# Loads between passes in order of need, one weight's conversion in the third pass, and Strassen products that accumulate on a copy in PSUM

## The chip, the cores and the metric

One core of a Trainium2 chip runs the whole kernel. The metric is the device time of one execution in microseconds (us), as the median of three executions; less is better. The profile is of one more execution.

## What is computed

The reference is an attention layer without a score matrix, and two feed-forward layers behind it, all in float32 accuracy (the inputs arrive as 64-bit floats):

```python
kv = einsum('bhsd,bhse->bhde', softmax_over_s(k), v)      # 8 batches, 8 heads, 576 x 64
x  = einsum('bhsd,bhde->bhse', softmax_over_d(q), kv)     # -> 4608 tokens x 512
h  = x @ moe_w_in;   g = h * sigmoid(1.702 * h);  x = g @ moe_w_out      # 512 -> 2048 -> 512
h  = x @ moe2_w_in;  g = where(h >= 1, h, where(h <= -1, 0, (h + 1)**2 / 4))
out = g @ moe2_w_out
```

## The kernel before

The program has four stages, one behind the other, and TensorE (PE) carries each.

**Stage 1** (nine blocks of 512 tokens, 16 steps `s` in each, 144 in all) does the attention and the first product, `x @ moe_w_in`. Each step is `gemm1`, 12 matmuls; every second step `act` takes two PSUM banks, applies the sigmoid on ScalarE (ACT) and the multiplication on VectorE (DVE), and stores the result in `g0_dram`. Beside it, at steps that a table of `at(step, function)` sets, run the softmaxes of the next block and the **conversion of the three remaining weights** (`out1`, `in2`, `out2`): of each weight four sets, each with two loads of raw 64-bit data, two conversions, and the seven operand sums of a Strassen-Winograd scheme, each split into a high and a low part (`hi`, `lo`) and stored in `wp_dram[weight, p]`, p = 1 to 7. There are 12 sets, ten steps apart.

**Pass 0** (`pass_out(0, "out1")`), **pass_in** (`"in2"`) and **pass 1** (`pass_out(1, "out2")`) then multiply by those weights in seven products a block instead of eight. Tokens come in five blocks j of twice 464 or 460. The activations of a block are four quadrants, "11", "12", "21" and "22"; `operand` forms each product's operand in place on DVE, `split` makes `hi` (an ACT copy) and `lo` (a DVE subtraction), and `gemm` issues 12 matmuls for 128 x 2 rows of it: in pass 0 and pass 1 a product has four such steps, in pass_in one for each of four column groups g. `post` combines the products. Before, PSUM holds three accumulators `z`: products 1 and 2 add up in one, 5 and 3 in a second, 6, 7 and 4 in a third, and the rest of the Winograd sums (`s1`, `v`, `u2`) is done by DVE with SBUF tiles.

Each pass needs seven weight tiles of 2 MB (`w`, from `wp_dram`), in the seven slots of `wpool`; stage 1 holds the same slots with its own weight (4) and the conversion's scratch (3). It needs the first block's quadrants as well: 16 tiles `gq` in pass 0 and 1 (four to a quadrant, 464 KB each), 4 tiles `xq` in pass_in. All transfers are issued by SyncE (SP), one after the other: an issue that waits for a free tile or for a finished result holds back all that stand behind it. A scheduler reorders the instructions of each engine by its own estimates; the rows under *The change* show what it made of each kernel. In the kernel before each pass begins with

```python
sl = load_weights(wname)             # all seven weights
...
for qd in ("11", "12", "22", "21"):  # then the quadrants
    load_g(0, qd)
```

Of the kernel before, what the change touches and what calls it, by code (L numbers as in the profile page):

```python
# [18 lines left out]
def kernel(  # L19
# [42 lines left out]
    PROD = (1, 5, 6, 2, 7, 3, 4)  # L62
# [38 lines left out]


    with ExitStack() as st0:
        vpool = st0.enter_context(tc.tile_pool(name="va", bufs=1))
        xpool = st0.enter_context(tc.tile_pool(name="x", bufs=2))
# [5 lines left out]
        sm = st0.enter_context(tc.tile_pool(name="sm", bufs=2))  # L111
        sgp = st0.enter_context(tc.tile_pool(name="sg", bufs=4))
# [31 lines left out]

        f12 = (s_f[:, 0:1024], s_f[:, 1024:2048])
        f_r = s_f[:, 2048:3072].bitcast(U32)
        f_s = s_f[:, 3072:3584]
        hl_n = [0]
        w_srcs = {"out1": w1_out, "in2": w2_in, "out2": w2_out}

        def load_set(w, si, i):
            raw = s_raw[:, i * 2048:(i + 1) * 2048].bitcast(I64)
            src = w_srcs[w]
            if w == "in2":
                c0 = i * (DFF // 2) + si * 256
                nc.sync.dma_start(
                    out=raw.rearrange("p (k f) -> p k f", k=KD),
                    in_=src[:, c0:c0 + 256].rearrange("(k p) f -> p k f", p=P),
                )
            else:  # L160
                r0 = i * (DFF // 2) + si * 2 * P
                nc.sync.dma_start(
                    out=raw.rearrange("p (c f) -> p c f", c=2),
                    in_=src[r0:r0 + 2 * P, :].rearrange("(c p) f -> p c f", p=P),
                )

        def conv_set(i):
            conv(s_raw[:, i * 2048:(i + 1) * 2048].bitcast(I64), f12[i], f_r)

        def quads(w):  # L170
            if w == "in2":
                v4 = [f.rearrange("p (k f) -> p k f", k=KD) for f in f12]
                return v4[0][:, 0:2], v4[0][:, 2:4], v4[1][:, 0:2], v4[1][:, 2:4]
            v2 = [f.rearrange("p (c f) -> p c f", c=2) for f in f12]
            return v2[0][:, :, 0:256], v2[1][:, :, 0:256], v2[0][:, :, 256:512], v2[1][:, :, 256:512]

        def hl(w, si, p, src, neg=False):
            o = (hl_n[0] % 4) * 1024
            hl_n[0] += 1
            t = s_hl[:, o:o + 1024].bitcast(FP32R).rearrange("p (a c f) -> p a c f", a=2, c=2)  # L180
# [249 lines left out]
        for i in range(12):  # L430
# [5 lines left out]
            for part in range(4):  # L436
                at(s0 + 4 + part + 0.5, prep, w, si, part)
# [377 lines left out]
```

## Time and profile before

| | us |
|---|---|
| median of three executions (lowest 1729.0, highest 1732.06) | 1730.34 |
| the profiled execution | 1727.85 |
| its span (first to last instruction) | 1726.1 |
| PE busy | 1603.0 |
| DVE busy | 1234.0 |
| ACT busy | 874.1 |

The span is cut by three handoffs: stage 1 to pass 0 at about 561 us, pass 0 to pass_in at about 945, pass_in to pass 1 at about 1311. A row of the timeline says when an instruction started, how long it took, its engine, line and operands, and in brackets how long the engine had stood idle and what released it. A matmul's duration is longer than the distance to the next one, since they overlap.

### The profile page before, as it was taken

The page shows a single profiled execution, that of the slowest core. Times are in us where ns is not written, and L with a number is a line of the kernel's source. Part 1 is how long each engine was busy: PE and PEld are TensorE (multiplying, and loading weights), DVE is VectorE, ACT ScalarE, POOL GpSimd, SP SyncE. Part 2 cuts the span into 40 slices and gives each one's busy share as a digit, 9 for nine tenths or more (in the row PEclk, how much of TensorE's full clock was granted, in tenths as well). Part 3 has the DMA queues.
Part 4 walks back from the last instruction along what each step waited for, and adds up shares of the span by engine and source line. Part 5 has one row for each costly group of instructions (what it writes and reads, how often), then busy time and mean ns, then how long its engine had stood idle before and what let it go on. Part 6 is the DMA issues. An engine that isn't in the chain of part 4 may idle for free.

```text
span 1726.1 us, 20570 instructions
## 1 busy us (share of the span) xinstructions
PE 1603.0 (93%) x7584; PEld 1381.3 (80%) x7584; DVE 1234.0 (71%) x1541; ACT 874.1 (51%) x1037; POOL 9.3 (1%) x45
## 2 busy tenths in 40 slices
PE   5899999998999399999999899999993899999997
PEld 3678887876767288999998788998893789999997
DVE  7998887878784378687684575867752767768683
ACT  4866775656573144444443465655652344444443
POOL 0000000000000000000000000000000000000000
PEclk9999999999999699999999899999997899999999
DMA  8778888888788952725547433424239563442601
GB/s 213 219 250 283 272 271 262 277 263 252 238 296 330 396 165 90 208 80 151 164 156 271 157 125 131 162 99 159 97 114 371 231 185 98 139 140 80 197 23 44
DMA packets 240436, 330.60 MB, mean 192 GB/s; under 512 B 98384, under 2 KB 193616, under 8 KB 237648
## 3 DMA queue, kind: packets, MB, share of 16 engines
q1 hardware_dynamic: 240336, 329.30, 58.4%
q8 instruction: 59, 0.97, 0.2%
q14 instruction: 41, 0.34, 0.1%
HBM read 190.84 MB, written 138.41 MB: 191 GB/s over the span
## 4 chain that ended last, share of the span: by engine, by line
PE 67%; DMA 4%; DVE 2%; ACT 1%; issue 1%; SPq 0%; ACTq 0%; DVEq 0%
PE z L592 40%; PE z L720 20%; DMA gq<-g 3%; PE hps L383 2%; PE hps L385 1%; PE hps L384 1%; DMA xq<-x 1%; PE pt L615 1%; PE px L354 1%; DVE sg L392 0%; SPq L501 0%; ACT ga L737 0%; PE pk L305 0%; ACT ga L738 0%; DVE w L125 0%
## 5 line engine op out<-in xcount | busy, mean ns | idle before, releaser
L592 PE MATMUL z<-hi,w 128*128 128x460 f32 (+1 forms) x2240 | 658.2, 374 | 63.8 <-ACT hi L488 63.8
L592 PEld LDWEIGHTS z<-hi,w 128*128 128x128 f32 x2240 | 422.9, 189 | 112.3 <-ACT hi L488 64.6
L488 ACT ACTIVATE hi<-gq 128x920 fp32r<-128x920 f32 (+1 forms) x280 | 273.0, 975 | 452.5 <-PE z L592 367.0
L489 DVE TENSOR_TENSOR lo<-gq,hi 128x920 fp32r<-128x920 f32 (+1 forms) x280 | 312.1, 1115 | 214.5 <-ACT hi L488 213.4
L592 PE MATMUL z<-lo,w 128*128 128x460 f32 (+1 forms) x1120 | 417.3, 373 | 0.8 <-DVE lo L489 0.8
L720 PE MATMUL z<-hi,w 128*128 128x460 f32 (+1 forms) x1120 | 327.6, 373 | 3.5 <-ACT hi L488 2.3
L383 PE MATMUL hps<-xh,w 128*128 128x512 f32 x576 | 237.1, 412 | 7.3 <-ACT w L124 3.5
L720 PEld LDWEIGHTS z<-hi,w 128*128 128x128 f32 x1120 | 211.7, 189 | 29.0 <-ACT hi L488 2.6
L592 PEld LDWEIGHTS z<-lo,w 128*128 128x128 f32 x1120 | 212.3, 190 | 25.2 <-DVE lo L489 1.7
L385 PE MATMUL hps<-xh,w 128*128 128x512 f32 x576 | 230.5, 400 | 1.1 <-DVE w L125 1.1
L384 PE MATMUL hps<-xl,w 128*128 128x512 f32 x576 | 229.4, 398 | 0.0
L720 PE MATMUL z<-lo,w 128*128 128x460 f32 (+1 forms) x560 | 209.3, 374 | 6.5 <-DVE lo L489 6.5
L492 DVE TENSOR_TENSOR gq<-gq 128x920 f32<-128x920 f32 (+1 forms) x160 | 175.9, 1113 | 2.1
L383 PEld LDWEIGHTS hps<-xh,w 128*128 128x128 f32 x576 | 109.1, 190 | 35.7 <-ACT w L124 5.5
L385 PEld LDWEIGHTS hps<-xh,w 128*128 128x128 f32 x576 | 109.0, 189 | 27.6 <-DVE w L125 2.2
L384 PEld LDWEIGHTS hps<-xl,w 128*128 128x128 f32 x576 | 109.1, 189 | 24.3 <-issue 0.6
L720 PEld LDWEIGHTS z<-lo,w 128*128 128x128 f32 x560 | 106.3, 190 | 19.2 <-DVE lo L489 7.2
L392 DVE TENSOR_TENSOR sg<-hps,sg 128x1024 f32<-128x1024 f32 x72 | 87.8, 1219 | 33.6 <-ACT sg L391 33.4
L391 ACT ACTIVATE sg<-hps 128x1024 f32<-128x1024 f32 x72 | 73.8, 1025 | 68.5 <-PE hps L385 68.0
L738 ACT ACTIVATE ga<-ga 128x920 f32<-128x920 f32 (+1 forms) x80 | 77.8, 973 | 2.1
L124 ACT ACTIVATE w<-w 128x512 fp32r<-128x512 f32 x88 | 54.5, 627 | 36.4 <-DVE w L98 20.7
L125 DVE TENSOR_TENSOR w<-w 128x512 fp32r<-128x512 f32 x88 | 59.3, 683 | 6.2 <-ACT w L124 6.0
(78 smaller groups left out, 1362.6 us busy)
## 6 DMA issues: line engine op xcount, KB each, us to landing
g<-sg SPq DMA_DIRECT2D x72, 512.0 KB
gq<-g SPq DMA_DIRECT2D x72, 460.0 KB
g<-ga SPq DMA_DIRECT2D x64, 460.0 KB
wp_out<-w SPq DMA_DIRECT2D x56, 512.0 KB
w<-wp_out SPq DMA_DIRECT2D x14, 2048.0 KB
w<-in_moe_w_out_dram SPq DMA_DIRECT2D x16, 1024.0 KB
wp_in<-w SPq DMA_DIRECT2D x28, 512.0 KB
w<-wp_in SPq DMA_DIRECT2D x7, 2048.0 KB
```

The lines of the kernel that those rows point to most:

```text
L125: nc.vector.tensor_tensor(out=lo, in0=src, in1=hi.bitcast(FP32), op=ALU.subtract)
L383: nc.tensor.matmul(out=hps, lhsT=wh, rhs=xh[:, kk, :], start=(kk == 0), stop=False)
L384: nc.tensor.matmul(out=hps, lhsT=wh, rhs=xl[:, kk, :], start=False, stop=False)
L385: nc.tensor.matmul(out=hps, lhsT=wl, rhs=xh[:, kk, :], start=False, stop=(kk == KD - 1))
L391: nc.scalar.activation(out=sg, in_=hps, func=ACTF.Sigmoid, scale=1.702)
L392: nc.vector.tensor_tensor(out=sg, in0=hps, in1=sg, op=ALU.mult)
L488: nc.scalar.activation(out=hi, in_=src, func=ACTF.Copy)
L489: nc.vector.tensor_tensor(out=lo, in0=src, in1=hi.bitcast(FP32), op=ALU.subtract)
L492: nc.vector.tensor_tensor(out=o, in0=x, in1=y, op=op)
L592: nc.tensor.matmul(out=z[:, m, :n], lhsT=a, rhs=b[:, c, :], start=(p in OPENS and i == 0 and c == 0 and x == 0), stop=(i == 3 and c == 1 a ...
L720: nc.tensor.matmul(out=z[:, m, :n], lhsT=a, rhs=b[:, c, :], start=(p in OPENS and c == 0 and x == 0), stop=(c == 1 and x == 2), skip_group ...
L738: nc.scalar.activation(out=t, in_=t, func=ACTF.Square)
```

## The change

1. **Order of loads.** `load_weights` is gone. Three weights of pass 0 (products 1, 7, 6) are loaded from step 113 of stage 1 on, into the scratch slots. In each `pass_out` quadrants and weights alternate in the order of use: "11", 1, 7, "12", "22", 6, 2, "21", 5, 4, 3. In pass_in the quadrants stand ahead of the weights. Pools are opened in another order, which moves tiles in SBUF: in pass_in the operands `c` lie ahead of the results `o`, in stage 1 `x` lies behind the small tiles.
2. **Conversion.** The four sets of `out2` leave stage 1; its eight other sets stand 12 steps apart instead of 10. In pass_in eight sets of half the width (128 rows) stand 14 gemms apart, with one raw buffer, three store buffers and seven output tiles instead of eleven.
3. **Products.** The order is 1, 7, 6, 2, 5, 4, 3. Product 1 stays in `z` and takes 2 on top; ACT also copies it into a second PSUM tile `zx`, on which 6, 5 and 3 accumulate in turn, and each state of `zx` is read once: `u2` behind 6, a sum with `s7` behind 5, the result behind 3. Products 7 and 4 accumulate in a third tile. Five DVE additions become two, one ACT copy out of product 1 becomes one into PSUM and more into SBUF. `widen` writes each `zx` buffer once with two matmuls of 512 columns at the start of a pass.

```diff
-    PROD = (1, 5, 6, 2, 7, 3, 4)
+    PROD = (1, 7, 6, 2, 5, 4, 3)
...
-        for i in range(12):
+        for i in range(8):
             w, si = MATS[i // 4], i % 4
-            s0 = NM + 1 + i * 10
+            s0 = NM + 1 + i * 12
...
+        for p in PROD[:3]:
+            at(NM + 8 * 12 + 1, load_weight, first_w, "out1", p)
...
+    def widen(pool, w, n):
+        for _ in range(n):
+            z = pool.tile([P, 2, TB], FP32, tag="zx", name="zx")
+            for b in range(2):
+                nc.tensor.matmul(
+                    out=z[:, b, :], lhsT=w[:, 0, 0, :P], rhs=w[:, 0, 0, :], start=True, stop=True,
...
-            zpool = pool("z", 4, space=bass.MemoryType.PSUM)
+            zpool = pool("z", 3, space=bass.MemoryType.PSUM)
+            zxpool = pool("zx", 1, space=bass.MemoryType.PSUM)
...
-            for qd in ("11", "12", "22", "21"):
-                load_g(0, qd)
+            for what in ("11", 1, 7, "12", "22", 6, 2, "21", 5, 4, 3):
+                if isinstance(what, str):
+                    load_g(0, what)
+                elif what not in sl:
+                    load_weight(sl, wname, what)
+            widen(zxpool, sl[1], 1)
...
             xp = pool("x", 4)
-            op = pool("o", 11)
             cp = pool("c", 14)
-            zpool = pool("z", 4, space=bass.MemoryType.PSUM)
+            op = pool("o", 7)
+            pp = pool("pp", 1)
+            zpool = pool("z", 2, space=bass.MemoryType.PSUM)
+            zxpool = pool("zx", 2, space=bass.MemoryType.PSUM)
...
                 if p == 1:
-                    tmp[g, "s1"] = new("s1")
-                    nc.scalar.activation(out=tmp[g, "s1"], in_=z, func=ACTF.Copy)
+                    zs[g, "x"] = zxpool.tile([P, 2, TB], FP32, tag="zx", name="zx")
+                    nc.scalar.activation(out=zs[g, "x"][:, :, :n], in_=z, func=ACTF.Copy)
+                elif p == 7:
+                    tmp["s7"] = keep("s7")
                 elif p == 6:
-                    tmp[g, "u2"] = new("u2")
-                    tt(tmp[g, "u2"], tmp[g, "s1"], z, ALU.add)
+                    tmp["u2"] = keep("u2")
                 elif p == 2:
                     finish(z, 0, 0)
+                elif p == 5:
+                    tt(tmp["s7"], tmp["s7"], z, ALU.add)
+                    finish(tmp["s7"], 1, 1)
```

SP at the end of stage 1, before. `g0_8_6` and `g0_8_7` are the last two results of stage 1, `w_...<-wp_out1` the weights of pass 0, `gq_...<-g0` the quadrant tiles ("11" first: the four with 464 columns).

```order
L501 DMA w_4787<-wp_out1_5_66 128x4096
L393 DMA g0_8_6_156<-sg_4741 128x1024
L501 DMA w_4789<-wp_out1_6_67 128x4096
L393 DMA g0_8_7_157<-sg_4770 128x1024
L501 DMA w_4791<-wp_out1_2_68 128x4096
L501 DMA w_4793<-wp_out1_7_69 128x4096
L501 DMA w_4795<-wp_out1_3_70 128x4096
L501 DMA w_4797<-wp_out1_4_71 128x4096
L557 DMA gq_4811<-g0_0_0_86 128x2x464
L557 DMA gq_4813<-g0_0_1_87 128x2x464
L557 DMA gq_4815<-g0_0_2_88 128x2x464
L557 DMA gq_4817<-g0_0_3_89 128x2x464
```

The same place after the change:

```order
L412 DMA g0_8_4_154<-sg_4549 128x1024
L183 DMA w_4710<-wp_out1_4_70 128x4096
L412 DMA g0_8_5_155<-sg_4578 128x1024
L412 DMA g0_8_6_156<-sg_4607 128x1024
L569 DMA gq_4666<-g0_0_0_86 128x2x464
L569 DMA gq_4668<-g0_0_1_87 128x2x464
L412 DMA g0_8_7_157<-sg_4636 128x1024
L569 DMA gq_4670<-g0_0_2_88 128x2x464
L569 DMA gq_4672<-g0_0_3_89 128x2x464
L569 DMA gq_4674<-g0_0_0_86 128x2x48
L569 DMA gq_4674<-g0_1_0_94 128x2x416
L569 DMA gq_4677<-g0_0_1_87 128x2x48
```

Three weights have left this place for earlier ones (not shown), and the first two quadrant tiles stand ahead of stage 1's last store instead of behind seven weights.

SP at the end of pass_in, before. `g1_4003` to `g1_4103` are the stores of the last column group, `w_...<-wp_out2` the weights of pass 1, `gq_...<-g1_0000` on the first quadrant.

```order
L742 DMA g1_4003_245<-ga_9936 256x1x460
L742 DMA g1_4013_249<-ga_9954 256x1x460
L742 DMA g1_4113_257<-ga_9972 256x1x460
L501 DMA w_10003<-wp_out2_6_81 128x4096
L742 DMA g1_4103_253<-ga_9990 256x1x460
L501 DMA w_10005<-wp_out2_2_82 128x4096
L501 DMA w_10007<-wp_out2_7_83 128x4096
L501 DMA w_10009<-wp_out2_3_84 128x4096
L501 DMA w_10011<-wp_out2_4_85 128x4096
L551 DMA gq_10028<-g1_0000_178 128x928
L551 DMA gq_10030<-g1_0001_179 128x928
L551 DMA gq_10032<-g1_0002_180 128x928
```

The same place after the change:

```order
L772 DMA g1_4102_252<-ga_9986 256x1x460
L183 DMA w_10154<-wp_out2_1_79 128x4096
L772 DMA g1_4012_248<-ga_10003 256x1x460
L183 DMA w_10156<-wp_out2_7_80 128x4096
L772 DMA g1_4003_245<-ga_10064 256x1x460
L772 DMA g1_4113_257<-ga_10082 256x1x460
L772 DMA g1_4103_253<-ga_10100 256x1x460
L772 DMA g1_4013_249<-ga_10117 256x1x460
L563 DMA gq_10146<-g1_0000_178 128x928
L563 DMA gq_10148<-g1_0001_179 128x928
L563 DMA gq_10150<-g1_0002_180 128x928
L563 DMA gq_10152<-g1_0003_181 128x928
```

The weights of products 1 and 7 now stand between the stores of the column group before the last; no weight is left between the last store and the quadrants, of which "11", "12" and "22" follow one another, and the weights of 6 and 2 come behind those.

ACT in pass_in, one column group of a block in the middle, before: `L746` copies product 1, `L737` and `L738` are the two steps of the activation function (four quadrants a group).

```order
L746 ACTIVATE s1_8138<-z_8125 128x2x460
L737 ACTIVATE ga_8168<-s1_8010,half_64 128x2x460
L738 ACTIVATE ga_8168<-ga_8168 128x2x460
L737 ACTIVATE ga_8200<-z_8125,half_64 128x2x460
L738 ACTIVATE ga_8200<-ga_8200 128x2x460
L737 ACTIVATE ga_8218<-u2_8186,half_64 128x2x460
L738 ACTIVATE ga_8218<-ga_8218 128x2x460
L737 ACTIVATE ga_8236<-v_8153,half_64 128x2x460
L738 ACTIVATE ga_8236<-ga_8236 128x2x460
L746 ACTIVATE s1_8254<-z_8241 128x2x460
```

After the change, column group 1 of the first block: `zx` is the copy into PSUM, `s7` and `u2` are copies out of PSUM, `pf` and `ph` belong to the conversion of a set (`L91` converts, `L103` and `L150` split), `L767` and `L768` are the activation function.

```order
L781 ACTIVATE zx_7537<-z_7524 128x2x464
L91 ACTIVATE pf1_7336<-praw_7334 128x512
L776 ACTIVATE s7_7552<-z_7539 128x928
L103 ACTIVATE ph1_7340<-ps_7338 128x256
L150 ACTIVATE ph2_7341<-pf1_7336 128x256
L103 ACTIVATE ph0_7339<-ps_7338 128x256
L776 ACTIVATE u2_7566<-zx_7537 128x928
L767 ACTIVATE ga_7580<-z_7524,half_64 128x928
L103 ACTIVATE ph1_7340<-pf1_7336 128x256
L768 ACTIVATE ga_7580<-ga_7580 128x928
L103 ACTIVATE ph2_7341<-pf0_7335 128x256
L103 ACTIVATE ph0_7339<-pf1_7336 128x256
```

A group has 11 ACT instructions of its own instead of 9, and the conversion's stand between them; the activation function of product 2 (`ga_7580`) is the eighth row from the copy of product 1 on.

## Rows read from the trace of the kernel before

**Rows 1.** The page, engines over the whole span: busy us (share) xinstructions.

```profile
PE 1603.0 (93%) x7584; PEld 1381.3 (80%) x7584; DVE 1234.0 (71%) x1541; ACT 874.1 (51%) x1037; POOL 9.3 (1%) x45
```

**Rows 2.** Timeline of PE, first handoff: start, us, engine, line, operands [idle <-releaser].

```profile
560.21 0.40 PE L385 MATMUL hps<-xh,w 128*128 128x512 f32 x1
...
590.46 0.75 PE L592 MATMUL z<-hi,w 128*128 128x464 f32 x1 [29.86 <-ACT hi L488]
```

**Rows 3.** Windows there: from:to, us, PE PEld DVE ACT POOL, PE clock, DMA, GB/s.

```profile
565.00:590.00 25.00, 0.00 (x0) 0.00 (x0) 0.00 (x0) 0.57 (x1) 0.00 (x0) 0.52 1.00 417
...
594.00:596.00 2.00, 2.00 (x6) 1.70 (x6) 1.80 (x2) 0.17 (x1) 0.00 (x0) 0.50 1.10 340
...
598.00:600.00 2.00, 2.00 (x11) 1.80 (x10) 1.83 (x3) 0.98 (x1) 0.00 (x0) 1.00 1.09 343
```

**Rows 4.** Timeline of DVE, end of pass 0: the sums behind its last two products.

```profile
935.23 1.12 DVE L492 TENSOR_TENSOR u<-u,z 128x920 f32<-128x920 f32 x1 [0.60 <-PE z L592]
...
945.25 1.11 DVE L492 TENSOR_TENSOR s<-s,z 128x920 f32<-128x920 f32 x1 [7.88 <-PE z L592]
```

**Rows 5.** Timeline of PE, second handoff: pass 0's last matmul, and pass_in.

```profile
944.84 0.37 PE L592 MATMUL z<-hi,w 128*128 128x460 f32 x1
...
958.59 0.76 PE L720 MATMUL z<-lo,w 128*128 128x464 f32 x1 [5.86 <-DVE lo L489]
```

**Rows 6.** Timeline of PE, third handoff: pass_in's last matmul, pass 1's first.

```profile
1310.73 0.37 PE L720 MATMUL z<-hi,w 128*128 128x460 f32 x1
1345.00 0.75 PE L592 MATMUL z<-hi,w 128*128 128x464 f32 x1 [33.90 <-ACT hi L488]
```

**Rows 7.** Timeline of SP, third handoff: last store, four weights, first quadrant tiles.

```profile
1315.88 0.51 SPq L742 DMA_DIRECT2D g<-ga  x1
1316.48 2.46 SPq L501 DMA_DIRECT2D w<-wp_out  x4
1319.04 0.96 SPq L551 DMA_DIRECT2D gq<-g  x2
```

**Rows 8.** Timeline of ACT, pass 1: copies that wait for quadrant tiles.

```profile
1346.23 0.98 ACT L488 ACTIVATE hi<-gq 128x928 fp32r<-128x928 f32 x1 [0.21 <-DMA gq<-g]
1347.38 0.98 ACT L488 ACTIVATE hi<-gq 128x928 fp32r<-128x928 f32 x1 [0.18 <-DMA gq<-g]
```

**Rows 9.** Groups by line and shape, ACT: count | busy us, mean ns | idle before.

```profile
L488 ACT ACTIVATE hi<-gq 128x920 fp32r<-128x920 f32 x224 | 218.1, 974 | 324.0 <-PE z L592 304.3 <-DVE lo L489 12.3 <-DMA out_dram<-u 4.6
L391 ACT ACTIVATE sg<-hps 128x1024 f32<-128x1024 f32 x72 | 73.8, 1025 | 68.5 <-PE hps L385 68.0
...
L124 ACT ACTIVATE w<-w 128x512 fp32r<-128x512 f32 x88 | 54.5, 627 | 36.4 <-DVE w L98 20.7 <-DVE w L196 11.3 <-DMA wp_in<-w 1.9
...
L737 ACT ACTIVATE ga<-u,half 128x920 f32<-128x920 f32 x16 | 17.1, 1066 | 33.6 <-DVE u L492 33.6
...
L746 ACT ACTIVATE s<-z 128x920 f32<-128x920 f32 x16 | 14.7, 921 | 0.0
L91 ACT ACTIVATE w<-w 128x512 f32<-128x512 f32 x16 | 10.3, 666 | 6.8 <-DMA w<-in_moe_w_in_dram 6.7
```

**Rows 10.** The same view, DVE.

```profile
L489 DVE TENSOR_TENSOR lo<-gq,hi 128x920 fp32r<-128x920 f32 x224 | 249.4, 1113 | 130.6 <-ACT hi L488 130.1
L392 DVE TENSOR_TENSOR sg<-hps,sg 128x1024 f32<-128x1024 f32 x72 | 87.8, 1219 | 33.6 <-ACT sg L391 33.4
```

**Rows 11.** Windows, columns as in rows 3: two of stage 1, one of pass_in.

```profile
350.00:400.00 50.00, 44.31 (x210) 35.45 (x210) 41.54 (x78) 33.69 (x48) 1.23 (x4) 0.97 0.71 229
...
500.00:550.00 50.00, 46.69 (x185) 34.88 (x184) 32.99 (x46) 23.30 (x32) 0.00 (x0) 0.93 0.79 295
...
1000.00:1100.00 100.00, 100.00 (x478) 89.42 (x477) 73.42 (x70) 60.54 (x64) 0.00 (x0) 1.00 0.34 124
```

**Rows 12.** Timeline, first transfer of the program, and the DVE instruction that waits for it.

```profile
0.74 0.46 SPq L220 DMA_DIRECT2D kr<-in_k_dram  x1
...
3.73 0.43 DVE L270 TENSOR_TENSOR m<-kr 128x256 f32<-128x256 f32 x1 [3.73 <-DMA kr<-in_k_dram]
```

More of the change, by code (lines that the diff above doesn't have):

```diff
@@ L148, with split, tt, weight_sets @@
+    def split(hi, lo, src):
+        nc.scalar.activation(out=hi, in_=src, func=ACTF.Copy)
+        nc.vector.tensor_tensor(out=lo, in0=src, in1=hi.bitcast(FP32), op=ALU.subtract)
+    def tt(o, x, y, op):
+        nc.vector.tensor_tensor(out=o, in0=x, in1=y, op=op)
+    def weight_sets(width, raws, f12, f_r, f_s, hls):
+        w_srcs = {"out1": w1_out, "in2": w2_in, "out2": w2_out}
         hl_n = [0]
-        w_srcs = {"out1": w1_out, "in2": w2_in, "out2": w2_out}
-        def load_set(w, si, i):
-            raw = s_raw[:, i * 2048:(i + 1) * 2048].bitcast(I64)
+        def raw(i):
+            return raws[i % len(raws)].bitcast(I64)
+        def load(w, si, i):
@@ L763, in pass_in @@
-            for j in range(NJ):
-                for g in range(4):
-                    mine = [(j, g, p) for p in order]
-                    if seq:
-                        last = seq.pop()
-                        seq += mine[:2] + [last] + mine[2:]
-                    else:
-                        seq += mine
+                elif p == 5:
+                    tt(tmp["s7"], tmp["s7"], z, ALU.add)
+                    finish(tmp["s7"], 1, 1)
+                elif p == 4:
+                    tt(tmp["u2"], tmp["u2"], z, ALU.add)
+                    finish(tmp["u2"], 1, 0)
+                else:
+                    finish(z, 0, 1)
@@ L771, in pass_in @@
             load_x(0)
-            for p in order:
+            for p in PROD:
+                load_weight(sl, "in2", p)
+            widen(zxpool, sl[1], 2)
+            for p in PROD:
                 ready(0, p)
-            for j, g, p in seq:
-                if g == 0 and p == 3 and j + 1 < NJ:
+            jobs = {}
+            for i in range(8):
+                s0 = 14 + i * 14
+                for h in range(2):
+                    jobs.setdefault(s0 + 2 * h, []).append((load_set, ("out2", i, h)))
+                    jobs.setdefault(s0 + 2 * h + 1, []).append((convert_set, (h,)))
+                for part in range(4):
+                    jobs.setdefault(s0 + 5 + part, []).append((sum_set, ("out2", i, part)))
@@ L776, in pass_in @@
+            for s, (j, g, p) in enumerate((j, g, p) for j in range(NJ) for g in range(4) for p in PROD):
+                if g == 0 and p == 2 and j + 1 < NJ:
                     load_x(j + 1)
@@ L780, in pass_in @@
                     ready(j + 1, p)
+                for f, a in jobs.get(s, ()):
+                    f(*a)
     pass_out(0, "out1")
```

213 lines of the change are left out of this document (105 added, 108 removed).

## The prediction

> **What bounds the kernel now.** I read the page first. PE is busy for 1603.0 of 1726.1 us and no other engine comes near [rows 1]; in a window in the middle of pass_in PE is busy for all of it, with DVE at 73% and ACT at 61% [rows 11]. So inside a pass time falls only if PE has less to do, and it has not: the matmuls are the same. What can be won lies where PE stands still. The timeline of PE shows where: 29.86 us at the first handoff [rows 2], 33.90 us at the third [rows 6], both until the first operand's copy on ACT, and less at the second [rows 5].
>
> What does a handoff cost in all? Pass 0's last two products end 945.25 - 935.23 = 10.02 us apart [rows 4], so a step is 2.5 us, and a pass of 35 products (or 140 gemms) takes 350.7 us when nothing holds it. Stage 1 ends at 560.21 + 0.40 = 560.6, pass 0 at 944.84 + 0.37 = 945.2, pass_in at 1310.73 + 0.37 = 1311.1 [rows 2, 5, 6]. First handoff with pass 0: 384.6 - 350.7 = **33.9 lost**. Second with pass_in: 365.9 - 350.7 = **15.2 lost**. The first loss is 4.0 more than PE's idle time. Part of that is a slow start: between 594 and 596 us the granted clock is 0.50, at 598 it is 1.00 [rows 3], and matmuls then issue twice as fast. I take the same 4.0 behind the third: 33.9 + 4.0 = **37.9 lost**. Together 87 us.
>
> Why are the operands late? At the third handoff SP issues the last store at 1315.88, then four weights of 2 MB, and only at 1319.04 the first quadrant tile [rows 7]; the DMA engines are full meanwhile (share 1.00 in the like window of the first handoff, 417 GB/s [rows 3]). The first product needs one weight and one quadrant, but the quadrant stands behind all seven weights.
>
> **The change, part by part: first handoff.** Now three weights are loaded a block earlier, three more into slots that stage 1 gives up in its last block, and two tiles of quadrant "11" are issued ahead of the last store. With T the end of stage 1: ACT's last sigmoid takes 1.03 [rows 9], the first copy 0.97 behind it, so PE has its first `hi` at T + 2.0; DVE does 1.22 and 1.11 [rows 10], `lo` is there at T + 3.4. With the slow start of 4.0 that is 6.0. Next late could be product 7 (quadrants "12" and "22", 16 issues on SP): an issue costs some 0.6 us (2.46 for four [rows 7]), so the first tile of "22", the eleventh issue behind the last store at T + 2.4, is issued some 8.5 us behind T and there about 3 later, as the first transfer of the program needed 3.0 from issue to its reader [rows 12]. Two subtractions, a third that stands before it and a `lo` follow on DVE, 4.4 us: T + 16, just when product 1 ends (6.0 + 10.0). For that I add 0.5: 6.5 instead of 33.9, **-27.4**. Bounds: 4 (no slow start) and 14 (the "12" and "22" tiles late by as much again as they need to be issued).
>
> **Second handoff.** ACT's order has the last result's copy (0.92 [rows 9]) ahead of pass_in's first `hi` (0.97), since the second `widen` matmul pair waits for it too: PE starts at T + 2.2 instead of losing 15.2, plus 4.0 slow start: 6.2, **-9.0**. Bounds 3 and 10. The `widen` matmuls, eight in the whole kernel, take 0.2 to 0.4 us each and lie in these waits; without that cover they are 3 us.
>
> **Third handoff.** The last store stands where it stood, 1315.88 - 1311.1 = 4.8 us behind the last matmul, since the activation function of the last product must be finished first. "11" follows at once: first issue at T + 5.3, landing 3.0 later, copied by T + 9.3. With the slow start 13.3 instead of 37.9: **-24.6**. Product 7 needs the ninth tile; tiles land 1.15 us apart (two copies that waited for one, 1346.23 and 1347.38 [rows 8]), so T + 17.5, and with 4.4 us of DVE and ACT T + 22, while product 1 ends at T + 13.3 + 10 = 23.3. Weights follow at 2 MB in 5 us, one to each 10 us of PE. Here the Trainium skill speaks against the change ("DMA: Bandwidth & Descriptors", section "Where 436 GB/s comes from"): HBM gives a core about 358 GB/s. The trace has 417 [rows 3], so the measurement decides. By the page the tiles would be 1.3 us apart, the ninth at T + 18.7, and the sum would move by 0.2 us at the first tile. Bounds of this handoff, from rows alone: 11 and 23 (the first tile behind the 4 MB of two weights, 10 us).
>
> **Stage 1.** A third of the conversion leaves, and from step 113 on (about 474 us) none is left. PE lacks 5.7 us between 350 and 400 and 3.3 between 500 and 550 [rows 11]. The later loss falls where no set runs any more, of the earlier I take a third: **-5**. Bounds 0 and -9. The 6 MB of weights loaded there fill the DMA engines for 15 us; the last two `q` loads stand behind them, and DVE's order has their first use four steps on, which covers it.
>
> **Passes 0 and 1** lose three DVE additions and gain three ACT copies per block, 10 us per product and slack on both: nothing. Without that slack a copy would be 0.9 us, ten blocks, 28 us.
>
> **pass_in** is where the change costs. Four free accumulators become two and two, and PE now waits on ACT and DVE inside a group: product 6 for the copy into `zx`, product 5 for the copy `u2` out of it, product 3 for DVE's sum behind 5. Copies cost 0.92 (into PSUM no row shows one; I take the same), the two steps of the activation function 1.07 and, like a copy, 0.97 [rows 9]; a piece of 128x256 lies between half and all of the 0.63 of 128x512, I take 0.4. Walk a group with t = 0 at the end of product 1, gemms ending at 2.5, 5.0 and so on. ACT: `zx` to 0.9, a conversion (0.67 [rows 9]) to 1.6, `s7` when 7 is done 2.5 to 3.4, three pieces to 4.6, `u2` 5.0 to 5.9 (product 5 needs it at 7.5), product 2's function and three pieces 7.5 to 10.7. DVE finishes product 2 at 11.0, adds `s7` until 12.1; product 3 wants that at 12.5. ACT goes on with the other three results until 18.9, the next `zx` copy is done at 19.8, and the next product 6 wants it at 20.0. So it just fits, with 0.2 us to spare. In the last group of a block seven `hi` copies (6.8 us) and on DVE seven `lo` and four sums (12.2 us) come on top: ACT then has 20 us of work in 17.5, the `zx` copy is 2.2 late, the sum for product 3 about 1. That is 3.2 at each of four block ends, 13; for the 16 other groups with conversion I take 0.2 each, since every piece also waits for a store: **+16**. Bounds 0 (before, DVE has as much at a block's end and PE waits next to nothing) and 35 (one more function step, 1.07, in each of 17 groups).
>
> Sum: -27.4 - 9.0 - 24.6 - 5 + 16 = -50.0. The profiled execution took 1727.85, so 1677.9; the median before lies 2.5 above it: **1680**.
>
> **Rivals.** *pass_in without stalls*: the groups have their slack and block ends are absorbed, as before. For it: over a whole block ACT has work for 84% (four groups of 11.0 us, four half sets of 2.1 and 6.8 of copies, 59 of 70 us). Then 1664. *The loads are not early*: SP issues in order, and "11" still waits, behind a store that is late or 4 MB of weights on the full engines; handoffs one and three lose 7 and 10 more: 1697. *pass_in chained, slower than before*: each of 20 groups loses on `zx`, since the copy into PSUM is dear or a piece waits for its store at the head of ACT's queue, and PE's clock falls with each stop (0.50 after a standstill [rows 3]). At 4 us a group it costs 80 instead of 16: 1744; from 3.3 us a group on ((16 + 50) / 20) nothing is won. Against it: the walk above leaves 0.2 us, not minus 3. *The change moves nothing* (the first tiles wait as long, for another reason, in all three places) I give next to nothing: the rows show seven weights ahead of them, and these are gone.
>
> **Chances.** My forecast (1668 to 1692) 0.55, pass_in without stalls 0.18, late loads 0.15, something between late loads and the chain (pass_in costs 40 to 60) 0.06, the chain 0.04, no change 0.02. Range **1662 to 1706**: it takes in both neighbours and the bounds of pass_in. A difference of 0.2% (3.5 us) is about what a measurement tells here. Faster 0.94, same 0.02, slower 0.04.
>
> **What would show it.** Right: PE idle at the first and second handoff of 2 to 4 us each, at the third 8 to 10 with a quadrant tile as releaser; no PE wait inside passes 0 and 1; in pass_in PE waits on ACT's `zx` copy and on DVE's sum, 2 to 4 us near each block's end and little else; the clock at 0.50 behind each handoff. Wrong: PE waits in nearly every group of pass_in, or on conversion pieces; "22" late in pass 0 by more than 3 us; a third handoff over 15 us.

## The result, and the profile after

The changed kernel takes 1667.85 us (median of four executions, 1666.24 to 1669.16), the kernel before beside it 1731.2 (four, 1729.0 to 1735.96): ratio 0.963, 95% interval 0.9608 to 0.9652. The prediction said 1680 (1662 to 1706) and faster; the gain forecast was 50 us, the gain measured 63 in the medians and 60.0 between the two profiled spans (1726.1 and 1666.1).

The profile splits these 60 by stage. A stage ends with the end of its last matmul, read from PE's timeline; so each pass holds the handoff ahead of it, and pass 1 the end of the program.

| us | stage 1 | pass 0 | pass_in | pass 1 |
|---|---|---|---|---|
| before [rows 2, 5, 6] | 560.6 | 384.6 | 365.9 | 415.0 |
| after | 541.4 | 365.3 | 366.6 | 392.8 |
| measured difference | -19.2 | -19.3 | +0.7 | -22.2 |
| forecast | -5 | -27.4 | -9 + 16 = +7 | -24.6 |

The page's line of engines, after; PE has the same work as in [rows 1], ACT 73 us more, DVE 80 less:

```profile
PE 1602.8 (96%) x7592; PEld 1380.8 (83%) x7592; DVE 1154.3 (69%) x1519; ACT 947.5 (57%) x1155; POOL 8.1 (0%) x45
```

Windows of stage 1, before and after, from 110 us to its end (after, to 541), columns as in [rows 3]. PE lacked 13.0 of 450.6 us and now lacks nothing, at the full clock:

```profile
110.00:560.60 450.60, 437.58 (x2019) 348.62 (x2017) 359.54 (x617) 280.74 (x375) 5.30 (x20) 0.99 0.83 274
...
110.00:541.00 431.00, 431.00 (x2023) 347.22 (x2022) 309.83 (x550) 273.71 (x352) 4.01 (x20) 1.00 0.77 253
```

In pass_in, after, PE lacks 4.3 of 100 us, where [rows 11] lacked nothing:

```profile
1000.00:1100.00 100.00, 95.69 (x451) 84.41 (x452) 79.38 (x119) 77.09 (x107) 0.00 (x0) 1.00 0.73 246
```

Timeline of PE at the first handoff, which answers to [rows 2]: stage 1's last matmul, then every matmul that had to wait. Four waits, 8.8 us together, in place of one of 29.86; the last two are product 7's:

```profile
541.00 0.39 PE L404 MATMUL hps<-xh,w 128*128 128x512 f32 x1
...
545.00 0.48 PE L604 MATMUL z<-hi,w 128*128 128x464 f32 x1 [3.14 <-ACT hi L103]
548.52 0.76 PE L604 MATMUL z<-lo,w 128*128 128x464 f32 x1 [3.04 <-DVE lo L104]
...
562.87 0.48 PE L604 MATMUL z<-hi,w 128*128 128x464 f32 x1 [1.96 <-ACT hi L103]
564.03 0.76 PE L604 MATMUL z<-lo,w 128*128 128x464 f32 x1 [0.68 <-DVE lo L104]
```

DVE at the same place: the first `lo` stood behind a store of `sg`, product 7's subtraction behind a quadrant tile.

```profile
547.34 2.16 DVE L104 TENSOR_TENSOR lo<-gq,hi 128x928 fp32r<-128x928 f32 x2 [3.63 <-DMA g<-sg]
...
558.22 3.32 DVE L107 TENSOR_TENSOR gq<-gq 128x928 f32<-128x928 f32 x3 [4.67 <-DMA gq<-g]
```

PE at the second and the third handoff ([rows 5, 6]): the last matmul of a pass, `widen`, and the next pass's first product.

```profile
906.32 0.37 PE L604 MATMUL zx<-hi,w 128*128 128x460 f32 x1
...
909.89 0.48 PE L750 MATMUL z<-hi,w 128*128 128x464 f32 x1 [1.44 <-ACT hi L103]
...
1272.95 0.37 PE L750 MATMUL zx<-hi,w 128*128 128x460 f32 x1
1277.24 1.22 PE L534 MATMUL zx<-w 128*128 128x512 f32 x2 [3.91 <-DVE ga L769]
1284.49 0.76 PE L604 MATMUL z<-hi,w 128*128 128x464 f32 x1 [6.04 <-ACT hi L103]
```

SP at the third handoff, to be read against [rows 7]: one weight ahead of the last four stores, and no weight between these and the quadrants.

```profile
1260.82 0.33 SPq L183 DMA_DIRECT2D w<-wp_out  x1
1269.06 8.66 SPq L772 DMA_DIRECT2D g<-ga  x4
1277.82 9.46 SPq L563 DMA_DIRECT2D gq<-g  x12
```

Waits of PE in pass_in behind the handoff (window 915 to 1273): line, releaser, us in total, times, longest. Before there was one, of 1.2 us.

```profile
PE zx L750 <- ACT zx L781: 3.5, 5, 1.0
PE zx L750 <- DVE s L107: 2.4, 2, 1.5
PE zx L750 <- ACT u L776: 0.8, 1, 0.8
```

And ACT at one of them. A piece of the conversion (`ph`) waits 3.68 us at the head of ACT's queue until the store of an earlier piece has landed and frees its buffer; the copy `u2` stands behind it, and PE's product 5 waits for that at 1069.67:

```profile
1064.29 0.40 ACT L103 ACTIVATE ph<-ps 128x256 fp32r<-128x256 f32 x1
1068.37 0.42 ACT L103 ACTIVATE ph<-pf 128x256 fp32r<-128x256 f32 x1 [3.68 <-DMA wp_out<-ph]
1068.69 0.92 ACT L776 ACTIVATE u<-zx 128x920 f32<-128x920 f32 x1
```

### The profile page after: what moved, and what is told of

Read it like the earlier page. It is cut to its first block, busy times and chain, and to the rows that moved or that the text cites. A ratio compares the mean times of both kernels' runs of the same rounds, so it can differ in the third digit from the quotient of the medians.

```text
span 1666.1 us, 20831 instructions
## 1 busy us (share of the span) xinstructions
PE 1602.8 (96%) x7592; PEld 1380.8 (83%) x7592; DVE 1154.3 (69%) x1519; ACT 947.5 (57%) x1155; POOL 8.1 (0%) x45
## 4 chain that ended last, share of the span: by engine, by line
PE 86%; DMA 3%; DVE 3%; ACT 3%; issue 1%; SPq 0%; ACTq 0%; DVEq 0%
PE z L604 24%; PE zx L604 17%; PE z L750 8%; PE hps L402 8%; PE hps L404 8%; PE hps L403 8%; PE zx L750 7%; PE pk L324 2%; PE px L373 2%; PE pt L627 1%; ACT ga L767 1%; DMA wp_out<-ph 1%; PE pt L363 1%; DMA g<-ga 1%; DVE lo L104 1%
## 5 line engine op out<-in xcount | busy, mean ns | idle before, releaser
L103 ACT ACTIVATE hi<-gq 128x920 fp32r<-128x920 f32 (+1 forms) x280 | 272.3, 974 | 378.5 <-PE z L604 196.2
L604 PE MATMUL z<-hi,w 128*128 128x460 f32 (+1 forms) x1280 | 383.3, 376 | 11.1 <-ACT hi L103 11.1
L604 PE MATMUL zx<-hi,w 128*128 128x460 f32 (+1 forms) x960 | 285.2, 371 | 0.0
L604 PEld LDWEIGHTS z<-hi,w 128*128 128x128 f32 x1280 | 243.7, 190 | 40.6 <-ACT hi L103 12.7
L604 PE MATMUL z<-lo,w 128*128 128x460 f32 (+1 forms) x640 | 240.6, 376 | 4.4 <-DVE lo L104 4.4
L107 DVE TENSOR_TENSOR gq<-gq 128x920 f32<-128x920 f32 (+1 forms) x160 | 177.4, 1117 | 45.7 <-DMA gq<-g 42.3
L750 PE MATMUL z<-hi,w 128*128 128x460 f32 (+1 forms) x640 | 195.9, 373 | 1.4 <-ACT hi L103 1.4
L604 PEld LDWEIGHTS zx<-hi,w 128*128 128x128 f32 x960 | 180.1, 188 | 19.9
L604 PE MATMUL zx<-lo,w 128*128 128x460 f32 (+1 forms) x480 | 177.9, 371 | 0.0
L750 PE MATMUL zx<-hi,w 128*128 128x460 f32 (+1 forms) x480 | 149.9, 373 | 6.7 <-ACT zx L781 3.5
L604 PEld LDWEIGHTS z<-lo,w 128*128 128x128 f32 x640 | 122.3, 191 | 19.5 <-DVE lo L104 5.9
L750 PEld LDWEIGHTS z<-hi,w 128*128 128x128 f32 x640 | 120.8, 189 | 15.6 <-ACT hi L103 1.9
L404 PEld LDWEIGHTS hps<-xh,w 128*128 128x128 f32 x576 | 109.0, 189 | 27.4 <-DVE w L104 2.0
L750 PE MATMUL z<-lo,w 128*128 128x460 f32 (+1 forms) x320 | 119.4, 373 | 0.8 <-DVE lo L104 0.7
```

Of the source, the lines that this page charges most:

```text
L404: nc.tensor.matmul(out=hps, lhsT=wl, rhs=xh[:, kk, :], start=False, stop=(kk == KD - 1))
L604: nc.tensor.matmul(out=z[:, m, :n], lhsT=a, rhs=b[:, c, :], start=(p in OPENS and i == 0 and c == 0 and x == 0), stop=(i == 3 and c == 1 a ...
L750: nc.tensor.matmul(out=z[:, m, :n], lhsT=a, rhs=b[:, c, :], start=(p in OPENS and c == 0 and x == 0), stop=(c == 1 and x == 2), skip_group ...
```

## The experiments

All on the changed kernel unless the text says otherwise. Stage lengths are read as above, from each kernel's own trace.

| us | stage 1 | pass 0 | pass_in | pass 1 | median | ratio to before |
|---|---|---|---|---|---|---|
| changed kernel | 541.4 | 365.3 | 366.6 | 392.8 | 1667.85 | 0.9630 |
| b_no_out2 | 548.5 | 367.0 | 367.1 | 413.7 | 1702.01 | 0.9827 |
| a_sp10 | 550.9 | 366.1 | 365.8 | 391.8 | 1674.32 | 0.9663 |
| a_out2_back | 565.9 | 369.0 | 361.2 | 392.1 | 1688.86 | 0.9747 |
| a_no_conv | 540.9 | 365.3 | 359.7 | 392.8 | 1659.98 | 0.9584 |
| a_old_order | 542.3 | 372.0 | 372.2 | 417.6 | 1705.1 | 0.9840 |
| a_no_first_w | 541.4 | 365.3 | 363.7 | 392.1 | 1664.45 | 0.9608 |
| e_mix_sg | 542.6 | 370.6 | 365.1 | 391.1 | 1671.15 | 0.9646 |
| e_early11 | 539.8 | 366.4 | 366.8 | 387.1 | 1660.61 | 0.9586 |
| a_ph4 | 543.7 | 364.9 | 364.1 | 391.6 | 1662.69 | 0.9614 |
| a_old_prod | 542.5 | 360.6 | 359.9 | 400.3 | 1661.42 | 0.9602 |
| e_both | 541.6 | 362.5 | 364.1 | 384.6 | 1652.64 | 0.9553 |
| e_place | 538.7 | 361.7 | 364.9 | 384.1 | 1653.05 | 0.9558 |

The 95% intervals of the ratios reach 0.0013 to 0.0029 to either side. A trace is of one execution: that of b_no_out2 took 3.7 us less than the median, those of a_old_prod and a_ph4 3.6 and 3.4 more, and their stages add up to that execution. Kernels with the same stage 1 differ there by up to 5.0 us (538.7 to 543.7), and those with the same pass_in by up to 3.1 (363.7 to 366.8): a stage's length in one profile is no finer than that.

Both spreads have a place in the traces. Stage 1 varies in its start: from the 201st of the 1728 matmuls of `gemm1` to the last, all ten kernels with eight sets twelve steps apart take 433.0 to 433.4 us, the kernel before 453.4, a_out2_back 456.4, a_sp10 444.1 and b_no_out2 441.6. pass_in varies in part with the clock behind the second handoff: over the first 20 us of pass_in its mean is 1.00 in a_no_conv, a_no_first_w, e_mix_sg and e_both, 0.91 in the changed kernel and a_out2_back, 0.83 in e_early11. At half speed for the rest, 0.91 is worth some 1.8 us and 0.83 some 3.4 (an estimate).

**Stage 1: the third weight's sets, b_no_out2** (on the kernel before).

```diff
-        for i in range(12):
+        for i in range(8):
...
-    pass_out(1, "out2")
+    pass_out(1, "in2")
```

> The kernel before with the four sets of out2's conversion left out of stage 1, the eight others still ten steps apart; the third pass multiplies by in2's seven weights instead, so the output is another. Theory (the sets stand in the way of PE's k and q transposes only where their phase against the 16-step chain is bad, and the losses behind 400 us are those of out2): stage 1 ends about 13 us earlier than 560.6, the time is about 1718, and the window 350 to 400 still has PE at about 44 of 50 us. Rival 1 (the ten-step spacing is all): stage 1 as before, 1731. Rival 2 (out2's sets are all, also for the scheduler's order ahead of them): stage 1 ends at 541, 1712, no loss between 350 and 400.

Stage 1 ended at 548.5, 12.1 earlier, and 350 to 400 still lacked 4.8 us, as the theory had it. The time fell by 29, though, where the theory had 13: 17.6 more came from the first handoff, whose code the edit does not touch. PE's wait there was 13.37 instead of 29.86 us:

```profile
561.83 0.75 PE L592 MATMUL z<-hi,w 128*128 128x464 f32 x1 [13.37 <-ACT hi L488]
```

Without out2's sets the three scratch slots are free early, and SP's order takes three weights of pass 0 into stage 1 by itself (issued at 442.74, 449.15 and 457.58).

**Stage 1: the spacing, a_sp10.**

```diff
-            s0 = NM + 1 + i * 12
+            s0 = NM + 1 + i * 10
```

> The changed kernel with its eight sets ten steps apart instead of twelve. Theory (phase of the sets against the chain): stage 1 loses again what it lost between 350 and 400 us before, 6 to 8 us with the slow clock behind each wait: 1674 to 1676. Rival 1 (spacing is all): +19, 1687. Rival 2 (out2's sets are all): 1668, no change.

Stage 1 was 9.5 longer, the time 6.5: the theory's 6 to 8. One of the four executions took 1667.75, as the changed kernel does, and the intervals of the two ratios overlap (0.9634 to 0.9691 and 0.9608 to 0.9652), so the size of the time's change is not settled; the wait is in the trace. PE's loss between 350 and 400 is back (it is busy for 44.33 of 50 us). Here is one of its waits on PE, then DVE's rows ahead of it (the columns as in the timelines above):

```profile
393.42 0.66 PE L363 MATMUL pt<-ident,qt 128*128 128x128 f32 x4 [2.86 <-DVE qt L354]
```

```profile
388.89 0.69 DVE L351 TENSOR_REDUCE qz<-qt 128x8 f32<-128x512 f32 x1 [1.41 <-ACT qt L346]
389.49 1.22 DVE L94 SCALAR_TENSOR_TENSOR w<-w 128x1024 uint32<-128x1024 uint32 x1
390.63 0.17 DVE L352 TENSOR_SCALAR qz<-qz 128x8 f32<-128x8 f32 x1
390.81 1.23 DVE L98 SCALAR_TENSOR_TENSOR w<-w 128x1024 uint32<-128x1024 uint32 x1
391.95 0.20 DVE L353 RECIPROCAL qz<-qz 128x8 f32<-128x8 f32 x1
392.07 0.69 DVE L107 TENSOR_TENSOR w<-w 128x512 f32<-128x512 f32 x1
392.68 0.68 DVE L354 TENSOR_TENSOR qt<-qt,qz 128x512 f32<-128x512 f32 x1
```

The softmax of `q` needs four short instructions in a row (`qz`, `qz`, `qz`, `qt`); between them stand three of the conversion, L94, L98 and L107, 3.1 us together, and PE's transpose waits 2.86. DVE is hardly busier from 350 to 400 (41.61 us) than from 300 to 350 (40.66), where PE lost nothing; what costs is whose instruction stands in the gap. Here the wait costs more than itself, as the windows of PE behind it show (columns: from:to, us, PE busy, clock, DMA share, GB/s):

```profile
392.00:394.00 2.00, 0.58 (x5) 1.00 0.00 0
394.00:396.00 2.00, 2.00 (x7) 0.67 0.02 8
396.00:398.00 2.00, 2.00 (x7) 0.50 1.03 382
398.00:400.00 2.00, 2.00 (x12) 0.98 1.05 349
```

The granted clock falls to its lower level, 1.2 of 2.4 GHz, when PE is at work again, and PE issues 7 matmuls in 2 us instead of 12. But the kernel before has the same wait, 2.88 us at 393.62, behind the same full work, and its clock stayed up:

```profile
394.00:396.00 2.00, 2.00 (x12) 1.00 0.00 0
396.00:398.00 2.00, 2.00 (x11) 1.00 0.95 354
```

**All twelve sets back in stage 1, a_out2_back.**

```diff
-        for i in range(8):
+        for i in range(12):
             w, si = MATS[i // 4], i % 4
-            s0 = NM + 1 + i * 12
+            s0 = NM + 1 + i * 10
...
-            at(NM + 8 * 12 + 1, load_weight, first_w, "out1", p)
+            at(NM + 12 * 10 + 1, load_weight, first_w, "out1", p)
...
-            for i in range(8):
+            for i in range(0):
                 s0 = 14 + i * 14
```

> The changed kernel with all twelve sets back in stage 1, ten steps apart, and no conversion in pass_in; the three early weights are issued behind the last set, at step 137. Theory: stage 1 is 19 us longer (ends at about 560), pass_in gains back its stalls of 6.7 us of PE waits and the slow clock behind them, about 8: 1679. If stage 1's gain of 19 came from the earlier loads or the other layout of SBUF and not from the sets, it stays, and the time is about 1660. If conversion in pass_in costs nothing, 1687.

Stage 1 lost 24.5, more than the 19 it had gained, pass_in won 5.4, the first handoff lost 3.7. PE's waits in stage 1 are those of the kernel before again, nearly one by one (1.92 and 0.90 near 355 us, then 2.86, 1.98 and 2.63). So the sets are the cause of stage 1's gain, not SBUF; nor is it the early loads, which go out only from 443.55 us on in the changed kernel, behind most of these waits; all five end with a DVE instruction. That stage 1 is also 5.3 longer than in the kernel before has two sources in the traces: its first `gemm1` matmul starts 2.2 later (40.0 against 37.8), and the clock falls behind two waits where it stayed up before (0.83 from 394 to 404 and from 432 to 442, against 1.00 from 390 to 400 and from 428 to 438).

**No conversion of out2 at all, a_no_conv.**

```diff
-            for i in range(8):
+            for i in range(0):
                 s0 = 14 + i * 14
...
-    pass_out(1, "out2")
+    pass_out(1, "in2")
```

> The changed kernel without any conversion of out2 (neither in stage 1 nor in pass_in); the third pass multiplies by in2's seven weights instead, so the output is another. It prices the conversion in pass_in. Theory of the prediction (copies and pieces of the conversion crowd ACT and DVE at block ends): the 6.7 us of PE waits in pass_in and the slow clock behind them go, 1660. Rival (the stalls belong to the copy into PSUM and the fewer accumulators, whatever else runs): 1668, the waits on the zx copy and the sum stay.

1659.98: the theory, but for a rest. PE's waits in pass_in that remain are these, one at each block's first product 6:

```profile
PE zx L750 <- ACT zx L781: 2.2, 4, 0.6
```

So of 6.7 us of waits 2.2 belong to the copy into PSUM and 4.5 to the conversion. pass_in is 6.9 shorter, but some 1.8 of that is the clock behind the second handoff, which did not fall here; a_out2_back, where it fell as in the changed kernel and nothing is converted in pass_in either, won 5.4. The conversion in pass_in costs some 5 us, not 16.

**The order of loads, a_old_order and a_no_first_w.** The first puts all weights ahead of the quadrants again and takes out the job in stage 1; the second takes out the job alone.

```diff
-        for p in PROD[:3]:
-            at(NM + 8 * 12 + 1, load_weight, first_w, "out1", p)
...
-            for what in ("11", 1, 7, "12", "22", 6, 2, "21", 5, 4, 3):
+            for what in PROD + ("11", "12", "22", "21"):
```

> The changed kernel with the loads in the old order: no weights loaded by a job of stage 1, in each pass all seven weights ahead of the quadrants. Theory 1 (the prediction's terms: the order alone is worth 27.4, 9.0 and 24.6 at the three handoffs): 1668 + 61 = 1729. Theory 2 (with out2's sets gone the scratch slots are free early and SP issues three weights early by itself, so that the first handoff costs 13.4 of idle time as in the run without out2's sets, some 5 more than in the changed kernel; the second and third cost 9 and 24 more): 1706.

> The changed kernel without the job that loads three weights of pass 0 at step 113; they are loaded in pass 0's own order of need. Theory 2: SP's order puts them into stage 1 all the same, since their slots are free there: 1668, within 3. Theory 1 (the job is what makes them early): two or three weights of 5 us each stand ahead of quadrants 12 and 22, 1678.

1705.1 and 1664.45: theory 2 in both, the second 0.6 beyond its 3. With the old order pass 0 is 6.7 longer, not 27.4, pass_in 5.6 and pass 1 24.8. The last is PE's wait for the first quadrant tile at the third handoff, 31.16 us where the changed kernel has 6.04, now that five weights stand between the last store and that tile:

```profile
1322.27 0.75 PE L602 MATMUL z<-hi,w 128*128 128x464 f32 x1 [31.16 <-ACT hi L103]
```

Without the job SP still issues three weights between 445 and 467 us (with it, at 443.55, 449.57 and 455.23). For the first handoff it does nothing: pass 0 is 365.3 in both. The kernel is 3.4 us faster without it, and that falls in pass_in (363.7), whose code is the same: the clock did not fall behind the second handoff, and PE's waits were 5.2 instead of 6.7 us. Why is not shown.

**The first handoff, e_mix_sg.** Two edits at once: the tiles of "12" and "22" in turn, and another place in SBUF for `sg`.

```diff
-        xpool = st0.enter_context(tc.tile_pool(name="x", bufs=2))
         sgp = st0.enter_context(tc.tile_pool(name="sg", bufs=4))
+        xpool = st0.enter_context(tc.tile_pool(name="x", bufs=2))
...
+                if what == "x":
+                    for i in range(4):
+                        load_g(0, "12", (i,))
+                        load_g(0, "22", (i,))
```

> The changed kernel with the first block's tiles of quadrants 12 and 22 loaded in turn, and with the sg tiles ahead of x in SBUF, so that pass 0's first lo no longer lies where the last sg tile is stored from. Theory (the first lo waits 3 us for that store, product 7 waits 2.6 us for the fourteenth issue of SP): PE's waits at the first handoff fall from 8.8 us to about 4, time 1663. Rival (product 7's hi stands behind the zx copy in ACT's order and ends the wait): the lo comes earlier but product 7 does not, 1668.

Neither: 1671.15, slower than the changed kernel by 3.3. Product 7's first operand came nearly in time (0.35 left, though its next two then waited 1.35 and 0.74), and PE had the first `lo` 1.2 behind the `hi`, but the first `hi` waited 11.65 instead of 3.14. With the moved tiles the order on SP is another one: the seventh weight now goes out ahead of all quadrant tiles, and the first two of these have lost their place ahead of the last store.

```profile
542.63 0.32 SPq L183 DMA_DIRECT2D w<-wp_out  x1
544.95 0.32 SPq L412 DMA_DIRECT2D g<-sg  x1
545.32 0.57 SPq L569 DMA_DIRECT2D gq<-g  x1
```

With one weight of 2 MB and the last store ahead of it, the first operand comes 8.5 us later, and pass 0 is 5.3 longer, since the other waits shrank: the prediction's mechanism at one place. Whether the first `lo` would still wait for `sg` can't be told, since its `hi`, at 553.69, came long after that store.

**The third handoff, e_early11.**

```diff
                 gemm(j, g, p)
+                if (j, g, p) == (NJ - 1, 2, 1):
+                    for i in range(4):
+                        t = qx.tile([P, 2, NX], FP32, tag="x", name="gq")
+                        nc.sync.dma_start(out=t[:, :, :HALVES[0]], in_=g1_dram[0, 0, 0, i])
+                        first_g.append(t)
```

> The changed kernel with pass 1's first quadrant 11 loaded inside the last block of pass_in, into the four x tiles, which are free there; the rest of the order stays. Theory (the third handoff waits for the first quadrant tile, which SP issues behind the last store and which lands 5.7 us later): PE's idle time there falls from 11.2 to about 4.2, time 1661. Rival (product 7 then waits for quadrants 12 and 22 instead): it gives 3 to 5 of the 7 back, 1664 to 1666.

The cut shows the load; the rest hands these four tiles to pass 1, whose `gq` pool has 12 tiles instead of 16. 1660.61: the theory, to the microsecond. PE's only wait before product 1 is the 3.91 ahead of `widen`; product 7 then waits 0.94 and 1.36.

**Store buffers in pass_in, a_ph4.**

```diff
-                [pp.tile([P, 512], FP32, name=f"ph{i}") for i in range(3)],
+                [pp.tile([P, 512], FP32, name=f"ph{i}") for i in range(4)],
```

> The changed kernel with four store buffers instead of three for the conversion pieces in pass_in. Theory (in pass_in a piece stands at the head of ACT's queue until an earlier piece's store has landed, 2.0 to 3.7 us, and the copy u2, the function of product 2 and so the sum for product 3 stand behind it): the waits of ACT on the store fall from 12 us to less than half, PE's waits inside pass_in from 9.2 to about 6, time 1665. Rival (ACT and DVE simply have too much work there): no change, 1668.

ACT's waits on the store fell by half, from 12.6 to 6.2 us, but 7.2 us of waits on the raw loads of the conversion came up in their place, and PE's waits went from 6.7 to 4.7. The median is 5.2 us lower with overlapping intervals, pass_in 2.5, within the spread of equal kernels: the direction agrees, the size is not settled.

**Products as before, a_old_prod** (compare a_no_conv: neither converts out2).

```diff
-    PROD = (1, 7, 6, 2, 5, 4, 3)
+    PROD = (1, 5, 6, 2, 7, 3, 4)
...
-            zpool = pool("z", 3, space=bass.MemoryType.PSUM)
-            zxpool = pool("zx", 1, space=bass.MemoryType.PSUM)
+            zpool = pool("z", 4, space=bass.MemoryType.PSUM)
...
                 if p == 1:
-                    zs["x"] = zxpool.tile([P, 2, TB], FP32, tag="zx", name="zx")
-                    nc.scalar.activation(out=zs["x"][:, :, :n], in_=z, func=ACTF.Copy)
+                    tmp["s1"] = new("s1")
+                    nc.scalar.activation(out=tmp["s1"], in_=z, func=ACTF.Copy)
```

> The changed kernel without out2's conversion (as in the run that left it out; the third pass multiplies by in2's weights) and with the products of before in all three passes: order 1, 5, 6, 2, 7, 3, 4, four free accumulators, five additions on DVE, no copy into PSUM, eleven output tiles in pass_in. Against that run (1660) it prices the third part of the change alone. Theory: products on a copy in PSUM move no time, since PE's work is the same: 1660, within 3. Rival 1 (the copy into zx holds PE up): faster by PE's five waits on it of 0.55 and the slow clock, 1655. Rival 2 (two additions less on DVE count): 1665.

1661.42 against 1659.98: no difference, and pass_in 359.9 against 359.7. But two differences in part cancel. Pass 0 is 4.7 shorter: product 5 stands second and needs "12" but not "22", and PE does not wait for it. Pass 1 is 7.5 longer, since in this kernel SP sends two more weights ahead of the quadrants:

```profile
1264.13 0.56 SPq L183 DMA_DIRECT2D w<-wp_in  x1
1267.80 0.51 SPq L753 DMA_DIRECT2D g<-ga  x1
1268.41 0.62 SPq L183 DMA_DIRECT2D w<-wp_in  x1
1269.12 20.33 SPq L559 DMA_DIRECT2D gq<-g  x16
```

**Both handoffs, e_both**: e_early11 and the turn of "12" and "22", with `sg` where the changed kernel has it.

> The run with quadrant 11 loaded inside pass_in, and the tiles of quadrants 12 and 22 loaded in turn in both out passes, SBUF as in the changed kernel (so the early issue of 11 ahead of the last store stays). Theory: product 7's waits of 2.6 us at the first and 2.3 at the third handoff go: 1660.6 - 4.5 = 1656. Rival (the wait moves to the later operands of product 7, whose tiles then come last): 1660.

1652.64, ratio 0.9553 (0.9538 to 0.9567): the fastest, 15 us below the changed kernel and 3 below the theory. Pass 0 gains 2.8 and pass 1 8.2 on it, which is what the cures add up to (product 7's 2.6; the 5.7 of e_early11 and product 7's 2.3). What is beyond the theory lies in pass_in (364.1 against 366.8 in e_early11), which the second cure does not touch: the clock behind the second handoff stayed at 1.00 where e_early11 has 0.83. Pass 1 now begins right behind `widen`:

```profile
1272.00 1.22 PE L534 MATMUL zx<-w 128*128 128x512 f32 x2 [3.91 <-DVE ga L780]
1273.02 0.59 PE L611 MATMUL z<-hi,w 128*128 128x464 f32 x1
```

**The place of the sets in pass_in, e_place** (on e_both).

```diff
-                s0 = 14 + i * 14
+                s0 = 11 + 28 * (i // 2) + 19 * (i % 2)
```

> The run with both handoffs mended (quadrant 11 inside pass_in, 12 and 22 in turn), and in pass_in the eight sets of out2's conversion moved within the block: their seven pieces fall 7 to 10 and 16 to 19 gemms behind a block's first, instead of 5 to 8 and 19 to 22, with the later one just ahead of the block's last group and the earlier one just behind its operands. Theory (a piece's wait on its store hurts where ACT and DVE are still behind from a block's seven hi copies and eleven operand operations): PE's waits in pass_in beyond the 0.55 at each block's first product 6 go, pass_in is 3 to 4 us shorter than 364.1 (without conversion it was 359.7), time 1649. Rival (a piece's wait costs as much wherever it falls): 1652.6, no change.

No change, but this does not speak for the rival: the edit did not move the work. On ACT the pieces stand in the same order as before it, only buffer numbers differ; the scheduler sends them early, whatever gemm they are written behind (in the changed kernel the last piece on ACT is at 1108 us, in the first 55% of pass_in). Whether another place would help was not tried in a form that tests it.

## Why the prediction was right, and where its sizes were off

**The mechanism held**: PE's work stayed, PE's standstill went, and the time fell by what the stages lost less. Three of the four terms were mis-sized; the errors are +14.2, -8.1, +6.3 and -2.4 us of gain, 10 in all. That the total came so near is in part luck: 20.5 us of gain too little were set against 10.5 too much.

*Stage 1* ("of the earlier I take a third: -5", bounds 0 and -9) failed most, and lay outside its bounds at -19.2. It read two windows and took part of their loss. PE lacked 13.0 us between 110 and 560.6 (450.6 less 437.6 busy). The lower clock came behind two of its groups of waits (mean 0.83 from 350 to 360 and 0.77 from 505 to 520), some 5 us more (an estimate, at half speed), and stayed away behind two others (1.00 from 390 to 400 and from 428 to 438). And it thought that losses stay where sets still run. a_sp10 shows that twelve steps in place of ten remove the loss between 350 and 400 altogether, with a small one near 293 us (9.5 in all), and b_no_out2 that out2's sets cost 12.1 by themselves.

*First handoff* ("6.5 instead of 33.9"): it lost 365.3 - 350.7 = 14.6, just beyond its bounds of 4 and 14. Two steps failed. With T the end of stage 1, the first `hi` came at T + 3.6 instead of 2.0, and the first `lo` at T + 7.1 instead of 3.4, since by the trace its subtraction waited for the store of the last `sg` tile; no run here takes that wait alone away. And "22" came later than worked out: DVE could begin product 7's operands 16.8 us behind T, not 11.5, and PE waited another 2.6 us, with the slow clock again; the prediction had named over 3 us there as a sign of error. An issue took 0.73 us (16.06 for 22), not 0.6, and by DVE's wait the tile was there 5 to 6 us behind its issue, not the 3.0 of the program's first transfer. The load order is also not alone in mending this handoff: out2's sets were in the way of the weights, and either cure does most of it (pass 0 is 367.0 with the old order and no sets of out2, 372.0 for the same with the new products, 369.0 with the new order and the sets in stage 1, 365.3 with both, 384.6 with neither).

*Second handoff and pass_in* (+7, measured +0.7). The order of loads is worth 5.6 here, 9.0 in the forecast. The "+16" of pass_in was 6.7 us of waits, of which the conversion brings 4.5. The walk through a group was right in its order and in which copies PE waits for, and wrong about the block's end: `zx` is 0.5 to 1.0 late there, not 2.2. It had also the mechanism that costs most, a piece that waits for its store at the head of ACT's queue, but under small change (0.2 a group); it strikes four groups for 0.6 to 1.5 each, 3.7 in all. The rest of the groups lose nothing. The walk had the conversion in all 20 groups; on ACT it was over in the twelfth.

*Third handoff* ("13.3 instead of 37.9", measured 2.4 more): idle 3.91 us ahead of `widen`, until the last result is read, and 6.04 until the copy of a quadrant tile, together in the 8 to 10 foretold. The first tile was issued 4.5 behind the end of pass_in, not 5.3, but ACT began its copy 5.65 later, not 3.0: the same landing time, taken from the program's start, was too short here (the DMA engines' share is 0.44 in the kernel before from 0.70 to 3.70, and 0.88 here from 1277.8 to 1283.5). e_early11 and a_old_order bear the mechanism out. The window 1284 to 1290 has the clock at 0.50 and moves 416 GB/s. The Trainium skill ("HBM Reference", section "Specifications (TRN2)") says that a core streaming alone gets well above its share of 358 GB/s, some 425. The trace agrees.

*Passes 0 and 1* "nothing", and products on a copy in PSUM nothing: a_old_prod agrees in its sum and in pass_in, apart from the loads that the order of products brings with it. It has no conversion in pass_in, though; whether the old products would leave room for that, as the new ones do, no run shows.

What stays open: how much of the conversion's some 5 us in pass_in another schedule could save, and why the clock falls behind the second handoff in some of these kernels and not in others.

## What to carry to other kernels

Price a stage by its own length against the work in it, not by the windows that catch the eye: one difference of two end points held the 13 us of waits and the slow clock behind some of them. PE's wait on a chain of short DVE instructions was cured here by moving what stood between them, at no less total work. And where one queue issues all transfers, look at what the first operand stands behind after each edit, also of SBUF layout or of the order of products: one weight more ahead of it and its place behind the last store made it 8.5 us later here. Take the time that a load needs to land from a moment when the engines are as full as they will be: 3.0 us at the program's start were 5.65 at the third handoff.

## What the runs showed of the hardware

In a_sp10 a wait of PE of 2.86 us, ahead of which it was busy throughout at the full clock (358 to 390 us), was followed by the lower clock, and the fall came when PE was already working again (0.67 and 0.50 in the two windows behind the wait, 0.98 after). In the kernel before a wait of 2.88 us at the same place, with PE as busy ahead of it, was followed by no fall (1.00 and 1.00). So the length of the wait and the work ahead of it do not settle by themselves whether the clock falls; what does, these traces do not show. The waits of 0.5 to 1.5 us in pass_in brought no fall: the window from 916 to 1273, which holds all eight, has 1.00.
